# A fourth expert by seven products, the side product first, and stored first-layer remainders in a fused attention and mixture-of-experts kernel

## The chip, the cores and the metric

The kernel runs on one core of a Trainium2 chip. The metric is the device time of one execution in microseconds (us). The engines are TensorE (PE, with its weight loads as PEld), VectorE (DVE), ScalarE (ACT), GpSimd (POOL) and SyncE (SP), whose queue issues nearly all DMAs here.

## The reference

Three parts follow each other on 1152 tokens of 512 features, all in float32:

```python
# attention: 2 x 8 heads, 576 keys, head size 64; only the 32 largest scores of a row are kept
scores = scale * np.matmul(q, k.transpose(0, 1, 3, 2))
kth = np.partition(scores, -top_k, axis=-1)[..., -top_k:-top_k + 1]
attn = softmax(where(scores >= kth, scores, -1e9));  x = attn @ v
# first MoE: 8 experts, 512 -> 1024 -> 512, gates by 8 rounds of row and column normalization
for e in range(E):
    h = np.maximum(x @ w1[e], 0.0)
    out += P[:, e:e + 1] * (h @ w2[e])
# second MoE: one wide layer, 512 -> 2048 -> 512
h = x @ w_in
g = h * np.tanh(softplus(h))
return g @ w_out
```

## The kernel before

Every float32 operand of a matmul is split in two parts, a rounded one (`hi`, type fp32r) and the remainder (`lo`), and a product is made of three: hi by hi, hi by lo, lo by hi. ACT rounds (L542), POOL or DVE subtracts (L546). A weight expert is cut in eight pieces of 128 hidden features; a piece has a first-layer half `wraw0` and a second-layer half `wraw1`, 256 KB each, fetched through SP (L533) into three buffers each. The parts `wl0` have four buffers, `wl1` five.

The nine token tiles of 128 go in three chunks: (0, 1), (2, 3) and the last, (4 to 8). Attention produces the tiles; the experts of chunks 0 and 1 run on PE between the attention of later tiles. When attention has ended, the last chunk (640 tokens) is done. `moe_chunk` goes over its experts: the first `PLAIN` = 5 by `ffn_pass` (plain), the other three by `pair_pass`.

Plain: a piece makes h in two column groups of 256 and 384 (12 matmuls each, L805), ACT and DVE make `hh` (Relu, L633) and `hl` (L634) of them, and two pieces later come the second-layer products (L679): five tiles of three matmuls of 512 columns. The two groups take turns in two PSUM banks `mm1`, each free again when its `hl` has been made.

By pairs: two pieces are taken as a 2 x 2 block matrix and multiplied with the tokens by seven products of half size (`Seven`, `load_pair`, `pair_pass`). A product is six matmuls of 320 columns (L711). Banks `run` and `alt` are the two `mm1`; the bank `side` has the tag `misc`, one buffer, which the transposes `x2t` use too. The order of PE in a pair is: 11 by 11 into `run`, ACT copies it (p1, L723); 12 by 21 into `side`, DVE adds p1 (`total`, L729), Relu and `hl`; carried second-layer products of earlier pieces; s2 by t2 on top of `run`; carried; s3, then s1 into `alt`; carried; 22; carried; s4. POOL makes the block sums of the weights (L569 to L573) and their remainders.

The remainders of second-layer weights are made once for some experts (`KEPT`), written to DRAM (L549) in chunks 0 and 1 and loaded instead of made in the last chunk (L544): experts 1 to 3 in chunk 0, experts 4 to 7 in chunk 1.

Other work of the last chunk stands in DVE's queue between these: 32 spilled rows of chunks 0 and 1 are loaded (L1022) and accumulated (L826); the weights of the second MoE come as float64 and are turned into float32 by integer steps (`double_to_float`, L954 to L961, 32 conversions, loads `cx` L947, writes `w<-cb` L962); the operands t1 to t4 of the pairs are made (`steps`), for the last chunk on POOL, for the second MoE on DVE. PE's order is the order of the program text. The other engines' orders are chosen by the planner from priorities (`st`) and a simulated time line; `after` adds an order without a wait. `pace` ties conversions and rows to the newest `hl` by counts of finished pieces, `follow` ties the DVE steps of the second MoE's operand to totals and `hl`.

Behind the last chunk comes the second MoE, units of four and five tiles, all by `pair_pass` with the function Mish.

Of the kernel before, what the change touches and what calls it, by code (L numbers as in the profile page):

```python
# [19 lines left out]
P = 128  # L20
# [30 lines left out]
FILL_FROM = 9  # L51
PLAIN = 5
PAIRS_FROM, TURN_FROM = 78, 126
DOUBLES, LEFT_RATE, SUMS = (7, 0.8, 0.4), 0.4, (7, 1.15)
KEPT = ((1, 2, 3), (4, 5, 6, 7))
# [23 lines left out]
def attention_moe_moe2(ctx: ExitStack, tc: tile.TileContext, qT, kT, vm, vt, wg, wst, w64, out):  # L79
# [458 lines left out]
    def parts(a, tag, raw, eng, n=DM, key=None):  # L538
        hi, lo = (
            wp.tile([P, DM], F32R, tag=f"w{k}{a}", name=f"w{k}{a}_{tag}", bufs=(4, LAG + 3)[a])[:, :n] for k in "hl"  # L540
        )
        live["rounded"] = nc.scalar.activation(hi, raw, AF.Copy)  # L542
        if key in low:
            nc.sync.dma_start(lo.bitcast(F32), low[key])  # L544
            return hi, lo
        eng.tensor_sub(lo, raw, hi)  # L546
        if key is not None and ps_b is None:
            low[key] = dram.tile([P, DM], F32, tag=f"low_{key[0]}_{key[1]}", name=f"low_{key[0]}_{key[1]}")
            nc.sync.dma_start(low[key], lo.bitcast(F32))  # L549
        return hi, lo  # L550

    def load_piece(tag, p, key):
        engines = nc.gpsimd, nc.vector if ps_b is not None else nc.gpsimd
        return [parts(a, tag, fetch_raw(a, tag, p), eng, key=key if a else None) for a, eng in enumerate(engines)]
# [67 lines left out]
    class Relu:  # L622
# [8 lines left out]
        def first(self, ps, c0, m):  # L631
            h, l = self.hh[:, c0 : c0 + m], self.hl[:, c0 : c0 + m]
            nc.scalar.activation(h, ps, AF.Relu)  # L633
            live["hl"] = nc.vector.scalar_tensor_tensor(l, ps, 0.0, h, op0=ALU.max, op1=ALU.subtract)  # L634
            if carry:
                follow(LEFT_RATE, live["hl"])
# [48 lines left out]
    def pair_pass(tag, tiles, pieces, x, act_class, finish):  # L685
# [40 lines left out]
        def total(bank, u, act, half, last=True):  # L726
            with st("first"):
                c = bank if last else tp.tile([P, m], F32, tag="c", name=f"c_{tag}_{g}", bufs=2)
                follow(1, nc.vector.tensor_add(c, bank, u))  # L729
                act.first(c, half * m, m)  # L730
# [6 lines left out]
        for g in range(nf // 2):  # L737
            with st("prep" if carry else "moe"):
                keys = [(tag[1:].partition("e")[2], 2 * g + i) if tag[0] == "c" else None for i in range(2)]
# [4 lines left out]
            )  # L744
            product(run, "11", "11", True)
            p1 = kept(run, "p1")
            side = ps_b.tile([P, 512], F32, tag="misc", name=f"hs_{tag}_{g}")[:, :m]
            product(side, "12", "21", True)
            total(side, p1, acts[0], 0)
            yield  # L750
# [22 lines left out]
    def ffn_pass(tag, tiles, pieces, xhi, xlo, act_class, finish):  # L773
# [19 lines left out]
        for f, p in enumerate(pieces):  # L793
            with st("prep" if pending else "moe"):
                ci, _, e = tag[1:].partition("e")
                keep = ps_b is not None or int(e) in KEPT[int(ci)]
                (w1h, w1l), w2 = load_piece(f"{tag}_{f}", p, (e, f) if keep else None)
# [209 lines left out]
    def pace(n):  # L1007

        first, rate, later = DOUBLES
        due = (min(n, PLAIN * EP) - first) * rate + max(n - PLAIN * EP, 0) * later  # L1010
        for kind, ahead in (("rows", n - FILL_FROM + 1), ("doubles", due + 1)):
            for group in paced[kind][held[kind] : max(int(ahead), 0)]:
                for inst in group:
                    after(inst, live["hl"])
                held[kind] += 1
# [21 lines left out]
    for i, _ in enumerate(moe_chunk(len(CHUNKS) - 1)):  # L1037
        next(gating, None)
        if live["hl"] is not last:
            last = live["hl"]  # L1040
            pieces += 1 if pieces < PLAIN * EP else 2 / 3
            pace(pieces)
            while sums and drawn < (pieces - SUMS[0]) * SUMS[1]:
                after(sums.pop(0), last)
                drawn += 1
        if i >= TURN_FROM and (i - PAIRS_FROM) % 8 in TURNS:
# [93 lines left out]
```

## Time and profile before

| | |
|---|---|
| time, median of 3 runs | 1196.35 us (1196.2 to 1196.69) |
| profiled execution, time | 1198.0 us |
| its span, first to last instruction | 1196.1 us |
| granted clock over the span | 0.994 |
| PE / DVE / ACT / POOL busy | 1150.1 / 926.4 / 712.8 / 704.3 us |
| read from HBM / written | 174.11 / 38.54 MB |

Matmuls are pipelined, so the span of one is longer than the step from one start to the next; both are used below and named. Times in rows are us from the span's start. A row of the timeline is start, duration, engine, line, operation, tiles, shape, and in brackets the idle time before it with what released it.

### The profile page before, as it was taken

To read this page: it belongs to the slowest core of one execution; us is meant where nothing else is said; L and a number is where in the kernel's file an instruction comes from. 1 tells how busy PE (TensorE), PEld (TensorE's weight loads), DVE (VectorE), ACT (ScalarE), POOL (GpSimd) and SP (SyncE) were. 2 spreads that over 40 slices of the span, in tenths; PEclk is the share of its full clock that TensorE was granted. 3 is DMA by queue.
4 is the path that set the end of the run, shared out by engine and by line. 5 is a ranking of instruction groups with operands and counts; after the bars stand their busy time and mean duration, and the time that the engine had idled before them with its cause. 6 is when DMAs were issued, how large, how long until landed. Compare 5 with 4: busy or idle time off the path is not lost.

```text
span 1196.1 us, 21441 instructions
## 1 busy us (share of the span) xinstructions
PE 1150.1 (96%) x7251; PEld 1025.3 (86%) x7251; DVE 926.4 (77%) x1943; ACT 712.8 (60%) x1454; POOL 704.3 (59%) x607
## 2 busy tenths in 40 slices
PE   3788999999999999999999999999999999999998
PEld 2566888898888999889999999998898989889997
DVE  7999999999999999943578888777666457886442
ACT  5877777777777777754233333333455546767653
POOL 6544877888777787762223343433665576787651
PEclk9998999999999999999999999999999999999999
DMA  8358777657565677754257776766454332233201
GB/s 254 106 180 280 237 258 232 187 162 226 177 214 169 214 235 231 242 174 158 81 175 246 247 256 222 268 209 229 164 177 141 125 114 80 97 107 115 96 29 45
DMA packets 121967, 214.08 MB, mean 179 GB/s; under 512 B 16000, under 2 KB 26496, under 8 KB 121856
## 3 DMA queue, kind: packets, MB, share of 16 engines
q1 hardware_dynamic: 120560, 211.52, 54.5%
q8 instruction: 57, 0.93, 0.3%
q10 hardware_dynamic: 1296, 1.18, 0.3%
q14 instruction: 54, 0.44, 0.1%
HBM read 174.11 MB, written 38.54 MB: 178 GB/s over the span
## 4 chain that ended last, share of the span: by engine, by line
PE 87%; DVE 3%; DMA 1%; ACT 1%; issue 1%; POOL 0%; SPq 0%; ACTq 0%; POOLq 0%
PE y_c2e L679 17%; PE h_c2e L805 11%; PE y_d L679 8%; PE h_c1e L805 8%; PE y_c1e L679 8%; PE h_c0e L805 6%; PE y_c0e L679 6%; PE h_d L711 6%; PE h_c2e L711 5%; PE pv L358 3%; PE tr L335 2%; PE sc L236 2%; PE pv L365 1%; PE hs_d L711 1%; PE hs_c2e L711 1%
## 5 line engine op out<-in xcount | busy, mean ns | idle before, releaser
L546 POOL TENSOR_TENSOR wl_c1e<-wraw_c1e,wh_c1e 128x512 fp32r<-128x512 f32 x128 | 171.2, 1348 | 60.2 <-ACT wh_c1e L542 56.9
L546 POOL TENSOR_TENSOR wl_c0e<-wraw_c0e,wh_c0e 128x512 fp32r<-128x512 f32 x112 | 148.3, 1337 | 51.1 <-ACT wh_c0e L542 44.1
L264 DVE MAX8 top<-w 128x8 f32<-128x576 f32 x216 | 158.5, 748 | 1.0
L546 POOL TENSOR_TENSOR wl_c2e<-wraw_c2e,wh_c2e 128x512 fp32r<-128x512 f32 x40 | 53.2, 1330 | 171.6 <-ACT wh_c2e L542 163.7
L542 ACT ACTIVATE wh_c2e<-wraw_c2e 128x512 fp32r<-128x512 f32 x80 | 50.6, 632 | 143.6 <-PE y_c2e L679 76.9
L542 ACT ACTIVATE wh_c1e<-wraw_c1e 128x512 fp32r<-128x512 f32 x128 | 80.5, 629 | 47.3 <-PE y_c1e L679 22.1
L271 DVE MATCH_REPLACE8 w<-top,w 128x576 f32<-128x576 f32 x144 | 106.6, 741 | 0.0
L805 PE MATMUL h_c2e<-xh,wh_c2e 128*128 128x256 f32 (+1 forms) x320 | 98.7, 308 | 0.6 <-DVE hl_c2e L634 0.6
L805 PE MATMUL h_c2e<-xl,wh_c2e 128*128 128x256 f32 (+1 forms) x320 | 98.2, 307 | 0.0
L805 PE MATMUL h_c2e<-xh,wl_c2e 128*128 128x256 f32 (+1 forms) x320 | 98.1, 307 | 0.0
L542 ACT ACTIVATE wh_c0e<-wraw_c0e 128x512 fp32r<-128x512 f32 x112 | 70.4, 629 | 46.1 <-PE y_c0e L679 15.6
L634 DVE SCALAR_TENSOR_TENSOR hl_c2e<-h_c2e,hh_c2e 128x256 fp32r<-128x256 f32 (+1 forms) x104 | 50.6, 487 | 53.8 <-ACT hh_c2e L633 53.6
L236 PE MATMUL sc<-ks,q 128*128 128x288 f32 x320 | 66.0, 338 | 23.6 <-POOL ks L168 5.5
L236 PEld LDWEIGHTS sc<-ks,q 128*128 128x128 f32 x320 | 53.1, 211 | 34.1 <-ACT early L249 7.4
L679 PE MATMUL y_c2e<-wh_c2e,hl_c2e 128*128 128x512 f32 x200 | 78.7, 394 | 0.0
L679 PE MATMUL y_c2e<-wl_c2e,hh_c2e 128*128 128x512 f32 x200 | 78.4, 392 | 0.0
L679 PE MATMUL y_c2e<-wh_c2e,hh_c2e 128*128 128x512 f32 x200 | 78.4, 392 | 0.0
L805 PE MATMUL h_c1e<-xh,wh_c1e 128*128 128x256 f32 (+1 forms) x256 | 76.4, 298 | 0.0
L665 DVE TENSOR_TENSOR hl_d<-mg_d,hh_d 128x256 fp32r<-128x256 f32 (+1 forms) x64 | 50.5, 796 | 32.4 <-ACT hh_d L664 32.0
L805 PE MATMUL h_c1e<-xh,wl_c1e 128*128 128x256 f32 (+1 forms) x256 | 73.3, 286 | 0.0
L805 PE MATMUL h_c1e<-xl,wh_c1e 128*128 128x256 f32 (+1 forms) x256 | 73.2, 286 | 0.0
L805 PE MATMUL h_c0e<-xh,wh_c0e 128*128 128x256 f32 x224 | 66.7, 298 | 1.1 <-DVE hl_c0e L634 0.9
(532 smaller groups left out, 3963.0 us busy)
## 6 DMA issues: line engine op xcount, KB each, us to landing
wraw_c1e<-in_wst_dram SPq DMA_DIRECT2D x128, 256.0 KB, 3.1
wraw_c0e<-in_wst_dram SPq DMA_DIRECT2D x112, 256.0 KB, 3.2
wraw_c2e<-in_wst_dram SPq DMA_DIRECT2D x80, 256.0 KB, 3.3
cx<-in_w_dram SPq DMA_DIRECT2D x32, 512.0 KB, 5.0
yd<-ysp SPq DMA_DIRECT2D x32, 256.0 KB, 3.6
low<-wl_c1e SPq DMA_DIRECT2D x32, 256.0 KB, 2.7
yb<-yd SPq DMA_DIRECT2D x32, 256.0 KB, 3.6
wl_c2e<-low SPq DMA_DIRECT2D x32, 256.0 KB, 3.8
```

The source lines that it names most:

```text
L236: nc.tensor.matmul(halves[half], q[:, h % HG, :], ks[b, h][:, half * HS : (half + 1) * HS], start=(i == 0), stop=(i == len(terms) - 1),)
L264: top8 = nc.vector.max(g, src)
L271: nc.vector.match_replace(w, g, src, NEG)
L335: nc.tensor.transpose(tr[:, c, :], em[:, j * D + c * P :][:, :P], ident)
L358: nc.tensor.matmul(pv[i * D : (i + 1) * D, pair, c0:c1], vmain[b, pair][:, i, c, :], live["at", i][:, c, c0:c1], start=(c == 0), stop=False,)
L542: live["rounded"] = nc.scalar.activation(hi, raw, AF.Copy)
L546: eng.tensor_sub(lo, raw, hi)
L634: live["hl"] = nc.vector.scalar_tensor_tensor(l, ps, 0.0, h, op0=ALU.max, op1=ALU.subtract)
L665: follow(LEFT_RATE, nc.vector.tensor_sub(l, g, h))
L679: nc.tensor.matmul(y, h[:, j * P : (j + 1) * P], w, start=(start and k == 0), stop=(stop and k == len(products) - 1))
L711: nc.tensor.matmul(bank, a[:, cols], b[:, c, :], start=(start and c + k == 0), stop=(c == 1 and k == 2), skip_group_check=not start,)
L805: nc.tensor.matmul(ps, w[:, c * P : (c + 1) * P], x[:, c, c0 : c0 + m], start=(k == 0), stop=(k == 3 * NC - 1),)
```

## The change

- `PLAIN` goes from 5 to 4: the last chunk makes experts 0 to 3 plain and 4 to 7 by pairs, sixteen pairs instead of twelve.
- `KEPT` has two entries per chunk, for the first-layer and the second-layer half. New is the first-layer half of experts 1 to 3, written in chunk 1 and loaded in the last chunk.
- In a pair the side product (12 by 21) stands before 11 by 11. This holds for the second MoE too.
- In the last chunk the DVE steps for the second MoE's operand are tied to the first `hl` of a pair only, three of them (`LEFT_PAIR`); conversions too are tied to that `hl` (`lead`) in the pairs. In the second MoE the old rule stays.
- The counts at which rows, conversions and POOL's sums are due become plans of several stretches (`due`). The transposes of the first rows begin at pair 5 instead of pair 6 and stand at two places of a pair instead of three.

```diff
--- before.py
+++ after.py
@@ -48,11 +48,11 @@
 EARLY_FROM, EARLY_STEPS = 5, 9
 HOLD, RATE = 8, 0.25
 ALONE, ALONE_RATE = 1, 3.4
-FILL_FROM = 9
-PLAIN = 5
-PAIRS_FROM, TURN_FROM = 78, 126
-DOUBLES, LEFT_RATE, SUMS = (7, 0.8, 0.4), 0.4, (7, 1.15)
-KEPT = ((1, 2, 3), (4, 5, 6, 7))
+PLAIN = 4
+PAIRS_FROM, TURN_FROM = 62, 102
+ROWS, DOUBLES, SUMS = ((8, 1.25),), ((7, 0.8), (32, 0.475), (48, 0.28)), ((7, 1.4),)
+LEFT_RATE, LEFT_PAIR = 0.4, 3.0
+KEPT = (((), (1, 2, 3)), ((1, 2, 3), (4, 5, 6, 7)))
 TURNS = (2, 4, 6)
 
 
@@ -545,13 +545,13 @@
             return hi, lo
         eng.tensor_sub(lo, raw, hi)
         if key is not None and ps_b is None:
-            low[key] = dram.tile([P, DM], F32, tag=f"low_{key[0]}_{key[1]}", name=f"low_{key[0]}_{key[1]}")
+            low[key] = dram.tile([P, DM], F32, tag=f"low{key[0]}_{key[1]}_{key[2]}", name=f"low{key[0]}_{key[1]}_{key[2]}")
             nc.sync.dma_start(low[key], lo.bitcast(F32))
         return hi, lo
 
     def load_piece(tag, p, key):
         engines = nc.gpsimd, nc.vector if ps_b is not None else nc.gpsimd
-        return [parts(a, tag, fetch_raw(a, tag, p), eng, key=key if a else None) for a, eng in enumerate(engines)]
+        return [parts(a, tag, fetch_raw(a, tag, p), eng, key=key[a]) for a, eng in enumerate(engines)]
 
     def load_pair(tag, pa, pb, keys):
 
@@ -632,8 +632,6 @@
             h, l = self.hh[:, c0 : c0 + m], self.hl[:, c0 : c0 + m]
             nc.scalar.activation(h, ps, AF.Relu)
             live["hl"] = nc.vector.scalar_tensor_tensor(l, ps, 0.0, h, op0=ALU.max, op1=ALU.subtract)
-            if carry:
-                follow(LEFT_RATE, live["hl"])
 
     class LateRelu(Relu):
 
@@ -726,7 +724,9 @@
         def total(bank, u, act, half, last=True):
             with st("first"):
                 c = bank if last else tp.tile([P, m], F32, tag="c", name=f"c_{tag}_{g}", bufs=2)
-                follow(1, nc.vector.tensor_add(c, bank, u))
+                total = nc.vector.tensor_add(c, bank, u)
+                if tag[0] == "d":
+                    follow(1, total)
                 act.first(c, half * m, m)
 
         def carried():
@@ -736,17 +736,20 @@
 
         for g in range(nf // 2):
             with st("prep" if carry else "moe"):
-                keys = [(tag[1:].partition("e")[2], 2 * g + i) if tag[0] == "c" else None for i in range(2)]
+                keys = [(1, tag[1:].partition("e")[2], 2 * g + i) if tag[0] == "c" else None for i in range(2)]
                 w, w2 = load_pair(f"{tag}_{g}", pieces[2 * g], pieces[2 * g + 1], keys)
             acts = [act_class(f"{tag}_{2 * g + i}", n) for i in range(2)]
             run, alt = (
                 ps_m.tile([P, 512], F32, tag="mm1", name=f"h_{tag}_{g}_{i}", bufs=2)[:, :m] for i in range(2)
             )
+            side = ps_b.tile([P, 512], F32, tag="misc", name=f"hs_{tag}_{g}")[:, :m]
+            product(side, "12", "21", True)
             product(run, "11", "11", True)
             p1 = kept(run, "p1")
-            side = ps_b.tile([P, 512], F32, tag="misc", name=f"hs_{tag}_{g}")[:, :m]
-            product(side, "12", "21", True)
             total(side, p1, acts[0], 0)
+            if tag[0] == "c":
+                live["lead"] = live["hl"]
+                follow(LEFT_PAIR, live["hl"])
             yield
             yield from carried()
             product(run, "s2", "t2", False)
@@ -793,8 +796,8 @@
         for f, p in enumerate(pieces):
             with st("prep" if pending else "moe"):
                 ci, _, e = tag[1:].partition("e")
-                keep = ps_b is not None or int(e) in KEPT[int(ci)]
-                (w1h, w1l), w2 = load_piece(f"{tag}_{f}", p, (e, f) if keep else None)
+                kept = [ps_b is not None or int(e) in KEPT[int(ci)][a] for a in range(2)]
+                (w1h, w1l), w2 = load_piece(f"{tag}_{f}", p, [(a, e, f) if kept[a] else None for a in range(2)])
             act = act_class(f"{tag}_{f}", n)
             for c0, m in groups(n):
                 with st("moe"):
@@ -1004,15 +1007,19 @@
     paced = {"rows": [], "doubles": []}
     held = dict.fromkeys(paced, 0)
 
-    def pace(n):
-
-        first, rate, later = DOUBLES
-        due = (min(n, PLAIN * EP) - first) * rate + max(n - PLAIN * EP, 0) * later
-        for kind, ahead in (("rows", n - FILL_FROM + 1), ("doubles", due + 1)):
-            for group in paced[kind][held[kind] : max(int(ahead), 0)]:
-                for inst in group:
-                    after(inst, live["hl"])
-                held[kind] += 1
+    def due(plan, n):
+
+        ends = [at for at, _ in plan[1:]] + [n]
+        return sum(max(min(n, end) - at, 0) * rate for (at, rate), end in zip(plan, ends))
+
+    def pace(n, inst):
+
+        for kind, plan in (("rows", ROWS), ("doubles", DOUBLES)):
+            if n >= plan[0][0]:
+                for group in paced[kind][held[kind] : int(due(plan, n)) + 1]:
+                    for each in group:
+                        after(each, inst)
+                    held[kind] += 1
 
     def once_gated():
 
@@ -1036,14 +1043,15 @@
     last, pieces, drawn = live["hl"], 0, 0
     for i, _ in enumerate(moe_chunk(len(CHUNKS) - 1)):
         next(gating, None)
-        if live["hl"] is not last:
-            last = live["hl"]
-            pieces += 1 if pieces < PLAIN * EP else 2 / 3
-            pace(pieces)
-            while sums and drawn < (pieces - SUMS[0]) * SUMS[1]:
+        mark = live["hl" if pieces < PLAIN * EP else "lead"] if "lead" in live else live["hl"]
+        if mark is not last:
+            last = mark
+            pieces += 1 if pieces < PLAIN * EP else 2
+            pace(pieces, last)
+            while sums and drawn < due(SUMS, pieces):
                 after(sums.pop(0), last)
                 drawn += 1
-        if i >= TURN_FROM and (i - PAIRS_FROM) % 8 in TURNS:
+        if i >= TURN_FROM and (i - PAIRS_FROM) % 8 in TURNS[:2]:
             next(first_rows, None)
     for _ in first_rows:
         pass
```

## Rows read from the trace of the kernel before

**Rows 1.** Page, busy us (share) and instructions of each engine

```profile
PE 1150.1 (96%) x7251; PEld 1025.3 (86%) x7251; DVE 926.4 (77%) x1943; ACT 712.8 (60%) x1454; POOL 704.3 (59%) x607
```

**Rows 2.** Page, chain that ended last, shares by engine

```profile
PE 87%; DVE 3%; DMA 1%; ACT 1%; issue 1%; POOL 0%; SPq 0%; ACTq 0%; POOLq 0%
```

**Rows 3.** Stretch, us, busy of PE, PEld, DVE, ACT, POOL, clock, DMA, GB/s

```profile
616.46:824.29 207.83, 207.26 (x1172) 188.31 (x1171) 166.28 (x256) 74.36 (x144) 75.32 (x64) 1.00 0.74 243
834.60:995.00 160.40, 160.08 (x889) 143.97 (x888) 95.67 (x163) 83.18 (x169) 97.70 (x96) 1.00 0.43 140
```

**Rows 4.** Timeline of PE, the same product of two plain pieces

```profile
664.76 0.34 PE L805 MATMUL h_c2e<-xh,wl_c2e 128*128 128x384 f32 x1
671.66 0.34 PE L805 MATMUL h_c2e<-xh,wl_c2e 128*128 128x384 f32 x1
```

**Rows 5.** Timeline of PE, the same product of two pairs in a row

```profile
899.27 0.31 PE L711 MATMUL h_c2e<-xh,wh_c2e_s 128*128 128x320 f32 x1
912.36 0.31 PE L711 MATMUL h_c2e<-xh,wh_c2e_s 128*128 128x320 f32 x1
```

**Rows 6.** Timeline at the border from plain to pairs: SP, DVE, PE

```profile
802.10 0.32 SPq L962 DMA_DIRECT2D w<-cb  x1
...
809.06 0.43 DVE L954 TENSOR_SCALAR cb<-cx 128x512 uint32<-128x512 uint32 x1 [2.65 <-DMA w<-cb]
...
810.71 1.75 DVE L959 SCALAR_TENSOR_TENSOR cb<-cx,cb 128x512 f32<-128x512 uint32 x1
...
814.01 0.39 PE L805 MATMUL h_c2e<-xh,wh_c2e 128*128 128x256 f32 x1 [0.57 <-DVE hl_c2e L634]
```

**Rows 7.** Timeline at the transposes x2t, and in an undisturbed pair (929)

```profile
916.46 0.83 DVE L961 SCALAR_TENSOR_TENSOR cb<-cd,cb 128x512 f32<-128x512 f32 x1
917.12 0.31 PE L711 MATMUL h_c2e<-t_c,wl_c2e_s 128*128 128x320 f32 x1
917.21 0.48 DVE L634 SCALAR_TENSOR_TENSOR hl_c2e<-hs_c2e,hh_c2e 128x320 fp32r<-128x320 f32 x1
917.75 0.66 PE L985 MATMUL x2t<-ident,acc 128*128 128x128 f32 x4 [0.32 <-DVE hl_c2e L634]
...
929.79 0.31 PE L711 MATMUL hs_c2e<-xh,wl_c2e 128*128 128x320 f32 x1
931.20 0.49 DVE L634 SCALAR_TENSOR_TENSOR hl_c2e<-hs_c2e,hh_c2e 128x320 fp32r<-128x320 f32 x1 [0.50 <-ACT hh_c2e L633]
```

**Rows 8.** Timeline in the second MoE: ACT's copy p1, s2, and a late hl

```profile
1041.67 0.38 ACT L723 ACTIVATE p_d<-h_d 128x256 f32<-128x256 f32 x1
1042.14 0.46 PE L711 MATMUL h_d<-t_d,wh_d_s 128*128 128x256 f32 x2
...
1044.01 0.51 PE L679 MATMUL y_d<-wh_d_3a,hl_d 128*128 128x512 f32 x1 [0.47 <-DVE hl_d L665]
```

**Rows 9.** Groups by line, 615 to 782 us: busy, mean ns, idle

```profile
L546 POOL TENSOR_TENSOR wl_c2e<-wraw_c2e,wh_c2e 128x512 fp32r<-128x512 f32 x24 | 32.3, 1347 | 104.4 <-ACT wh_c2e L542 99.7 <-DMA wl_c2e<-low 4.7
...
L826 DVE SCALAR_TENSOR_TENSOR acc<-yb,gate,acc 128x512 f32<-128x512 f32 x20 | 22.0, 1099 | 0.0
L954 DVE TENSOR_SCALAR cb<-cx 128x512 uint32<-128x512 uint32 x20 | 18.0, 899 | 0.5 <-DMA w<-cb 0.5
```

**Rows 10.** SP's waits from 300 to 560 us (total, times, longest); a stage

```profile
SPq L549 <- POOL wl_c1e L546: 43.1, 31, 3.6
...
480.00:500.00 20.00, 20.00 (x153) 17.91 (x153) 19.90 (x51) 15.25 (x31) 15.91 (x13) 1.00 0.70 226
```

**Rows 11.** A plain piece; GB/s in 40 slices of 797 to 818 us

```profile
671.66:678.56 6.90, 6.90 (x40) 6.28 (x40) 5.98 (x10) 2.59 (x5) 2.16 (x2) 1.00 0.83 264
...
GB/s 0 0 0 0 0 86 195 218 269 234 234 191 152 320 371 406 410 417 398 367 351 215 129 23 90 273 265 363 328 359 273 156 257 359 156 324 211 129 238 351
```

**Rows 12.** DMA issues (KB each, median us to landing): 797 to 818 us, whole span

```profile
w<-cb SPq DMA_DIRECT2D x3, 256.0 KB, 6.1
...
w<-cb SPq DMA_DIRECT2D x32, 256.0 KB, 4.1
```

## The prediction

> **What bounds the kernel now.** I read the page first: TensorE (PE) is busy for 96% of the span [rows 1] and the chain that ended last is 87% PE [rows 2]. Then the table by stage, because the change touches one stage above all: from 616 to 824 us, four of the five plain experts of the last chunk, PE is busy 207.26 of 207.83 us; from 834.6 to 995 us, the three experts made in pairs, 160.08 of 160.40 us, both at a granted clock of 1.00 [rows 3]. So time can come out of this stretch in two ways only: fewer PE columns, or the few gaps. Matmul spans overlap, so I took the pitch from start to start and not the mean duration, and went through all PE starts from 560 us to the end for places where the next product began later than its pitch allows. Three are large enough to count and can be touched by the change: 0.57 us at 814 by the idle time of the row [rows 6], 0.48 us at 917 (six products in a row end their pitch of 0.147 at 917.27, the transposes begin at 917.75) [rows 7], 0.47 us at 1044 [rows 8]. Each was released by VectorE (DVE), not by a load. DVE is not the bound by its share (77%) [rows 1], but its queue is in order, so one late instruction holds up the remainder `hl` that PE needs.
>
> The profiled execution took 1198.0 us (span 1196.1, 1.9 around it), 1.65 above the median 1196.35. The terms are differences inside the span, so I take them off the median.
>
> **Expert 4 by pairs.** A plain piece takes 6.90 us from one first product to the same product of the next piece [rows 4], two pieces 13.80. A pair of pieces takes 13.09 us [rows 5]: 42 products of 320 columns instead of 24 of 256 and 24 of 384, with the same second layer. Saved: 0.71 us a pair, four pairs, **2.84 us**, all on PE, which has no gap there to hide it in. For comparison, the isolated gap that the Trainium skill gives per matmul (TensorE: Matmul & The Clock Gate, section Back-to-back issue gap: N/2.4 + 2.5 ns) would make this an estimate of 0.82 us a pair, 3.3 in all; the rows show 0.71 and decide. What the pairs add runs elsewhere: three totals on DVE, three copies and one and a half more roundings on ScalarE (ACT), POOL's half-width sums and remainders. The three pair experts show that these fit: in 160.4 us DVE has 95.67 busy, ACT 83.18, POOL 97.70 [rows 3]. Cost zero, hidden under 13.09 us of products per pair; if that cover fails, the price is that of the rivals.
>
> **Remainders of the first layer kept (experts 1 to 3).** It removes 24 POOL subtractions, 32.3 us by the row of this stretch [rows 9]. POOL was not late for PE there, so this gains nothing directly. It adds 24 writes of 256 KB in chunk 1 and 24 loads of 256 KB in the last chunk, all on SP's in-order queue. A write waits for POOL's subtraction, and what stands behind it, mostly the next raw weights, waits too. The same write is there already for experts 4 to 7: SP waited for POOL 31 times, 43.1 us in all, longest 3.6, and in 480 to 500 us, inside these writes, PE was busy 20.00 of 20.00 us [rows 10]. So 24 new ones (about 1.4 us of SP time each) cost between nothing and one such wait, 3.6 us, if a prefetch comes late; I take nothing, since the raw buffers are three deep and the row for the same case shows no PE gap.
> The loads: the fullest plain piece shows a DMA share of 0.83 at 264 GB/s [rows 11]. 256 KB more in 6.90 us are 38 GB/s, a quarter of a spilled row 9.5: 0.98 in such a piece. That is near full, not beyond: the engines moved over 350 GB/s for 3.7 us from 804.3 us on [rows 11]. Raw weights and remainders are fetched some pieces ahead, so I take zero and keep the collision as a rival.
>
> **New pace of DVE work.** Spilled rows go at 1.25 a piece instead of 1 and end near piece 33, as they must, since the transposes of the first rows start at pair 5 of 16. DVE was busy 5.98 of 6.90 us in a full piece [rows 11]. A quarter row at 1.10 us adds 0.27. Against that, the first step of a conversion averages 0.90 us [rows 9], and 0.43 where it ran undisturbed [rows 6]; with 24 POOL subtractions less, up to 0.47 of this may return. So 5.8 to 6.25 us a piece: it fits, cost zero. In the pairs the conversions come at 0.95, later 0.56 a pair instead of 0.8, and the 24 steps for the second MoE's first operand at 3 a pair over eight pairs. Both are now ordered behind the lead `hl` of a pair, the one that frees bank `misc`. At 917 us the last step of a conversion ran between the pair's total and that `hl` [rows 7]; tied behind it, it cannot. I take the **0.48** off.
>
> **Side product first.** The copy p1 can now start only when the second product of the pair has ended, and total, Relu and `hl` come one copy (0.44 us) later. In an undisturbed pair the side product's last matmul starts at 929.79 and ends 0.31 later, and `hl` ends at 931.69, 1.6 us after it [rows 7]. With a copy in front that is 2.05. The next product into `run` begins 1.2 us after that point, behind six second-layer products of 0.23 us; the copy ends at about 0.5. It is hidden with 0.7 us to spare. The transposes `x2t`, which share `misc`, come behind s2 (six of 0.147 us), 2.1 us after it: no slack is left. Two sit there in this chunk and two in the next. Bounds: 0 and 0.45 us each. I take 0.1 for the two in this chunk, **+0.2**, and nothing for the other two, where the bank is released by Mish on ACT, before `hl`. The bank `run` gets 0.88 us more to come free, but nothing waited for it: zero.
> The gap at the border from plain to pairs (814 us) and the one at 1044 us I leave as they are: conversions are as dense before the border as they were, and the second MoE's DVE queue isn't touched.
>
> Sum: -2.84 - 0.48 + 0.2 = -3.1 us; 1196.35 - 3.1 = **1193.2**.
>
> **Rivals.** *All three gaps go* (-2.84 - 0.57 - 0.48 - 0.47 = -4.4, 1192.0): the border moves to a stretch in which POOL has no remainders to make. Against it: the pair's own preparation on POOL begins before the border in any case. Chance 0.15.
> *Given back by the later chain*: at 1041.67 us p1 was late and ended 0.09 us before s2 began [rows 8]. If that lag belongs to the copy, it will end one product later, 0.7 us (six of 256 columns, in proportion to 320), and s2 waits 0.6 us. Two such pairs and two full waits at the transposes (0.9 instead of 0.2) make 1.9: 1195.1, up to 1196.5 if more pairs are late. Against it: ACT's queue, not the product, made p1 late there, and that queue doesn't move. Chance 0.22, nearly all within 0.2%.
> *Slower: the fuller DMA queue holds up DVE in the plain pieces.* At 809 us the first step of a conversion waited 2.65 us for the write of an earlier one, issued at 802.10; a later step then took 1.75 us, and `hl` behind it came 0.57 us too late for PE [rows 6]. The median landing of that write was 6.1 us in this burst against 4.1 over the run [rows 12]. With up to 0.98 of the DMA taken this can happen at many of the 20 conversions before the border. It decides from five such events on (2.84/0.57) and is slower by over 0.2% from ten (5.5/0.57); with ten to fifteen, 1198.9 to 1201.8. Against it: in the fullest piece, DMA share 0.83, PE had no gap [rows 11]. Chance 0.11. The Trainium skill (SBUF — State Buffer, section Who interferes with whom) says that a DVE instruction with two SBUF inputs is blocked by a GpSimd instruction that reads SBUF; the 1.75 us agree, as POOL worked then. By that rule the 24 subtractions taken off POOL speak for the change, and the preparation of four more pairs against it.
> That the reordering and tying do nothing at all leaves 2.84: 1193.5, inside the forecast.
>
> **How the numbers follow.** Forecast 0.52, all gaps gone 0.15, given back 0.22, slower 0.11. A measurement of this kernel can tell 0.2%, 2.4 us: faster means under 1193.96. Of the forecast 0.04 lies above that. Faster 0.48 + 0.15 = 0.63; same 0.22 + 0.04 = 0.26; slower 0.11. The range runs from 1191.4 (all gaps gone and a little) to 1197.0, past the giving back, and leaves out the slower rival and a bit below.
>
> **What would show it.** Right: a pair period of 13.1 us sixteen times in the last chunk; that chunk about 3 us shorter, with the stretch up to 560 us unchanged; 24 `wl` loads more and no POOL remainders in experts 1 to 3; no gap over 0.2 us at `x2t`. Wrong: PE gaps in plain pieces released by `hl` with a DVE wait for `w<-cb` before it (the DMA rival); gaps before s2 released by p1 (the later chain); a first 560 us longer by more than 0.5 us (SP's new writes).

## The result, and the profile after

The changed kernel takes **1207.67 us** (median of 6 runs, 1205.79 to 1209.83); the kernel before takes 1196.79 us in the same comparison. The ratio is 1.0089 [1.0076, 1.0102]: slower by about 11 us, where 3.1 us faster had been forecast. The profiled execution took 1207.27 us (span 1205.5, granted clock 0.994, as before).

The page of the changed kernel, first the busy times [rows 1], then the shares of the chain that ended last [rows 2]:

```profile
PE 1149.0 (95%) x7227; PEld 1019.9 (85%) x7227; DVE 935.2 (78%) x1955; ACT 718.5 (60%) x1474; POOL 692.1 (57%) x607
...
PE 80%; DVE 11%; ACT 3%; DMA 3%; issue 2%; POOL 1%; SPq 0%; ACTq 0%; POOLq 0%; DVEq 0%
```

PE has hardly less to do, but the chain leaves it more often: DVE's share went from 3 to 11%, ACT's from 1 to 3%. Where, the table by stage tells (columns as in [rows 3]; the last chunk's gating, three plain experts, and the pairs):

```profile
560.00:617.00 57.00, 54.87 (x328) 49.74 (x328) 34.36 (x104) 16.75 (x36) 27.61 (x32) 1.00 0.41 132
617.00:780.00 163.00, 163.00 (x921) 148.35 (x920) 121.43 (x208) 58.90 (x115) 15.28 (x15) 1.00 0.85 284
781.00:1001.00 220.00, 213.29 (x1170) 189.98 (x1169) 157.46 (x234) 108.05 (x226) 133.13 (x126) 1.00 0.48 154
```

PE stands for 2.1 us in the gating stage, not at all in the plain experts, and for 6.7 us in the pairs, where the kernel before stood for 0.32 us in 160.4 [rows 3]. From the starts of PE's products I made a ledger of every kernel of this study. "Plain" runs from the first product of the last chunk to the first one of its first pair, "pairs" from there to the first product of the second MoE, "second" from there to the start of the last product; one profiled execution each, us. Time is the median over all runs of the kernel; the ratio is to the kernel before, run beside it on the same chip. A ledger row is one execution, which can lie off its kernel's median: e1's is the one at 1203.54 us, e7's the one at 1202.98.

| kernel | plain | pairs | second | time | ratio, 95% interval |
|---|---|---|---|---|---|
| before (5 plain, 12 pairs) | 275.35 | 159.49 | 197.38 | 1196.79 | 1 |
| changed (4 plain, 16 pairs) | 222.07 | 219.93 | 200.29 | 1207.67 | 1.0089 [1.0076, 1.0102] |
| e1_side_back | 221.93 | 220.50 | 197.39 | 1207.93 | 1.0091 [1.0058, 1.0123] |
| e2_no_first_kept | 219.31 | 219.64 | 200.40 | 1205.76 | 1.0074 [1.0058, 1.0090] |
| e3_no_conv_border | 221.94 | 213.95 | 199.67 | 1201.85 | 1.0045 [1.0030, 1.0060] |
| e4_side_only (12 pairs) | 274.65 | 163.26 | 201.49 | 1204.49 | 1.0062 [1.0044, 1.0080] |
| e5_three_undone | 219.31 | 218.23 | 197.34 | 1198.26 | 1.0014 [1.0005, 1.0024] |
| e6_kept_only (12 pairs) | 277.09 | 159.41 | 198.54 | 1199.56 | 1.0030 [1.0017, 1.0043] |
| e7_side_back_border | 221.90 | 219.61 | 197.32 | 1200.57 | 1.0032 [1.0019, 1.0045] |
| e8_four_old_pace | 219.31 | 218.00 | 198.22 | 1199.11 | 1.0026 [1.0014, 1.0038] |
| e9_no_late_conv | 219.36 | 210.93 | 197.60 | 1191.59 | 0.9959 [0.9944, 0.9974] |
| e10_kept_two (12 pairs) | 274.88 | 159.21 | 198.48 | 1195.98 | 0.9994 [0.9984, 1.0003] |
| e11_more_plain | 226.30 | 214.69 | 197.00 | 1200.88 | 1.0036 [1.0023, 1.0049] |
| e12_pool_steps | 230.22 | 219.00 | 197.35 | 1209.00 | 1.0099 [1.0083, 1.0116] |

Read against e9, in which PE's longest wait in these three parts is 0.32 us, the changed kernel loses 2.7 us in plain, 9.0 in the pairs, 2.7 in the second MoE. Waits of PE are given below from start to start, beyond the usual step of the matmul before. They come out about 0.15 us longer than the idle time in a row's brackets, because a matmul's span is longer than its step; for the same reason the busy times above show less than the 9.0 us.

**The pairs.** Groups of the conversion's six steps on DVE, changed kernel, 781 to 1000 us (columns as in [rows 9]; lines 957 to 964 are 954 to 961 of before), then the first step in the three pair experts of before, 834.6 to 995 us:

```profile
L964 DVE SCALAR_TENSOR_TENSOR cb<-cd,cb 128x512 f32<-128x512 f32 x12 | 14.4, 1204 | 0.6
L962 DVE SCALAR_TENSOR_TENSOR cb<-cx,cb 128x512 f32<-128x512 uint32 x12 | 13.9, 1161 | 0.4
L960 DVE SCALAR_TENSOR_TENSOR ca<-cx,cb 128x512 uint32<-128x512 uint32 x12 | 12.9, 1071 | 0.3
L963 DVE TENSOR_TENSOR cb<-ca,cb 128x512 f32<-128x512 f32 x12 | 9.5, 795 | 0.3
L961 DVE TENSOR_SCALAR cb<-ca 128x512 uint32<-128x512 uint32 x12 | 9.1, 762 | 0.3
L957 DVE TENSOR_SCALAR cb<-cx 128x512 uint32<-128x512 uint32 x12 | 8.9, 743 | 0.0
```

```profile
L954 DVE TENSOR_SCALAR cb<-cx 128x512 uint32<-128x512 uint32 x5 | 3.5, 697 | 0.0
```

Twelve conversions run in the pairs instead of six, counting in both kernels the one that lies astride the border (its first step falls ahead of the stretch of before, hence x5). They take 5.74 us each (the sum of the six means), 68.7 us of DVE. What this does to PE at a border between two pair experts, on the timeline of DVE, ACT, POOL and PE of the changed kernel:

```profile
837.34 0.49 DVE L634 SCALAR_TENSOR_TENSOR hl_c2e<-hs_c2e,hh_c2e 128x320 fp32r<-128x320 f32 x1 [0.50 <-ACT hh_c2e L633]
837.74 0.77 DVE L957 TENSOR_SCALAR cb<-cx 128x512 uint32<-128x512 uint32 x1
...
843.50 1.60 DVE L964 SCALAR_TENSOR_TENSOR cb<-cd,cb 128x512 f32<-128x512 f32 x1
845.02 0.48 DVE L727 TENSOR_TENSOR c_c2e<-h_c2e,u_c2e 128x320 f32<-128x320 f32 x1
845.42 1.39 DVE L829 SCALAR_TENSOR_TENSOR acc<-y_c2e,gate,acc 128x512 f32<-128x512 f32 x2
846.74 1.50 DVE L634 SCALAR_TENSOR_TENSOR hl_c2e<-c_c2e,hh_c2e 128x320 fp32r<-128x320 f32 x1
848.16 0.74 DVE L829 SCALAR_TENSOR_TENSOR acc<-y_c2e,gate,acc 128x512 f32<-128x512 f32 x1
848.82 0.47 DVE L634 SCALAR_TENSOR_TENSOR hl_c2e<-h_c2e,hh_c2e 128x320 fp32r<-128x320 f32 x1
...
840.65 0.44 ACT L721 ACTIVATE u_c2e<-h_c2e 128x320 f32<-128x320 f32 x1 [0.24 <-PE h_c2e L709]
...
846.61 1.29 POOL L546 TENSOR_TENSOR wl_c2e_s<-wraw_c2e_1b,wh_c2e_s 128x512 fp32r<-128x512 f32 x1 [2.05 <-PE h_c2e L709]
...
849.35 0.41 PE L709 MATMUL h_c2e<-xh,wh_c2e 128*128 128x320 f32 x1 [1.77 <-DVE hl_c2e L634]
```

Behind the lead `hl` comes a whole conversion (six steps, to 845.1). The total `c` needs the copy u (done at 841.09) and product s1 (its last matmul ends at 841.49), and runs at 845.02, some 3.5 us late. At this border the old expert's sums must be accumulated too (`acc`, 0.7 us each), and three of them stand ahead of the `hl` that frees bank `run`. Between them runs the `hl` of c, which takes 1.50 us itself, beside POOL's subtraction (last section). PE waits 1.92 us here, 1.82 at 907.61, 1.12 at 961.89, each followed by a late p1 (0.67, 0.66, 0.66). The other waits in the pairs are 0.54, 0.37 and 0.37 us at x2t. Together these make 8.1 of the 9.0 us.

No DVE instruction of these pairs waits 0.2 us or more for a DMA. In the six microseconds around the first border, and in those around 905 and 959 us, DVE is busy for 17.93 of 18.00 us:

```profile
844.00:850.00 6.00, 4.23 (x24) 3.55 (x24) 6.00 (x9) 2.14 (x5) 2.77 (x3) 1.00 0.55 192
```

**Gating.** First the changed kernel, then before: POOL's groups from 560 to 617 us and one step of DVE, for the changed kernel also POOL beside that step and the wait of PE:

```profile
L610 POOL TENSOR_TENSOR x_c<-xh,xl 128x320 f32<-128x320 f32 x8 | 7.3, 948 | 0.1
...
L546 POOL TENSOR_TENSOR wl_c2e<-wraw_c2e,wh_c2e 128x512 fp32r<-128x512 f32 x4 | 5.2, 1297 | 21.4 <-ACT wh_c2e L542 13.0 <-DMA wraw_c2e<-in_wst_dram 8.4
...
595.74 3.37 POOL L610 TENSOR_TENSOR x_c<-xh,xl 128x320 f32<-128x320 f32 x4
...
598.34 0.87 DVE L513 TENSOR_TENSOR gate<-gate,cr 128x72 f32<-128x72 f32 x1
...
600.81 0.41 PE L507 MATMUL cs<-gate,ones 128*128 128x72 f32 x2 [1.00 <-DVE gate L503]
```

```profile
L546 POOL TENSOR_TENSOR wl_c2e<-wraw_c2e,wh_c2e 128x512 fp32r<-128x512 f32 x8 | 10.4, 1295 | 45.9 <-ACT wh_c2e L542 42.8 <-DMA wraw_c2e<-in_wst_dram 3.1
L610 POOL TENSOR_TENSOR x_c<-xh,xl 128x320 f32<-128x320 f32 x2 | 1.7, 880 | 0.0
...
592.82 0.23 DVE L513 TENSOR_TENSOR gate<-gate,cr 128x72 f32<-128x72 f32 x1
```

Before, POOL's subtractions of the next weights waited 42.8 us for ACT, and POOL's sums x_c, which stand behind them in its queue, waited with them. Four of these subtractions are gone, so the sums run early, in the middle of the gating, and some of DVE's small steps beside them take several times as long (0.87 for 0.23 us). PE waits 0.34, 1.12 and 1.16 us for the gate.

**Second MoE.** ACT and PE, changed kernel; compare [rows 8]:

```profile
1071.75 0.61 ACT L542 ACTIVATE wh_d<-wraw_d_7a 128x512 fp32r<-128x512 f32 x1
1072.27 0.36 ACT L721 ACTIVATE p_d<-h_d 128x256 f32<-128x256 f32 x1
...
1072.69 0.50 PE L709 MATMUL h_d<-t_d,wh_d_s 128*128 128x256 f32 x2 [0.92 <-ACT p_d L721]
```

p1 now stands behind a rounding in ACT's queue, and s2 waits 1.09 us for it (0.80 at 1004.67). In the last unit a pair takes 13.20 to 13.24 us, against 13.05 to 13.10 with the old order (e1).

### The profile page after: what moved, and what is told of

Its sections match the earlier page's. It is cut to its first block, busy times and chain, and to the rows that moved or that the text cites. A ratio compares the mean times of both kernels' runs of the same rounds, so it can differ in the third digit from the quotient of the medians.

```text
span 1205.5 us, 21534 instructions
## 1 busy us (share of the span) xinstructions
PE 1149.0 (95%) x7227; PEld 1019.9 (85%) x7227; DVE 935.2 (78%) x1955; ACT 718.5 (60%) x1474; POOL 692.1 (57%) x607
## 4 chain that ended last, share of the span: by engine, by line
PE 80%; DVE 11%; ACT 3%; DMA 3%; issue 2%; POOL 1%; SPq 0%; ACTq 0%; POOLq 0%; DVEq 0%
PE y_c2e L677 16%; PE h_c2e L808 9%; PE y_d L677 7%; PE h_c1e L808 7%; PE y_c1e L677 7%; PE h_c0e L808 6%; PE y_c0e L677 6%; PE h_d L709 6%; PE h_c2e L709 5%; PE pv L358 2%; DVE top L264 2%; PE sc L236 2%; PE tr L335 2%; DMA kraw<-in_kT_dram 2%; DVE w L271 2%
## 5 line engine op out<-in xcount | busy, mean ns | idle before, releaser
L542 ACT ACTIVATE wh_c2e<-wraw_c2e 128x512 fp32r<-128x512 f32 x64 | 40.5, 633 | 116.3 <-PE y_c2e L677 63.0
L634 DVE SCALAR_TENSOR_TENSOR hl_c2e<-h_c2e,hh_c2e 128x256 fp32r<-128x256 f32 (+1 forms) x96 | 46.9, 489 | 59.4 <-ACT hh_c2e L633 59.3
L569 POOL TENSOR_TENSOR ws_c2e<-wraw_c2e_0a,wraw_c2e_0b 128x256 f32<-128x256 f32 x4 | 3.0, 752 | 148.5 <-DMA wraw_c2e_0b<-in_wst_dram 148.5
L663 DVE TENSOR_TENSOR hl_d<-mg_d,hh_d 128x256 fp32r<-128x256 f32 (+1 forms) x64 | 47.2, 737 | 50.3 <-ACT hh_d L662 49.9
L808 PE MATMUL h_c2e<-xh,wh_c2e 128*128 128x256 f32 (+1 forms) x256 | 78.9, 308 | 0.0
L808 PE MATMUL h_c2e<-xl,wh_c2e 128*128 128x256 f32 (+1 forms) x256 | 78.5, 307 | 0.0
L808 PE MATMUL h_c2e<-xh,wl_c2e 128*128 128x256 f32 (+1 forms) x256 | 78.5, 307 | 0.0
L633 ACT ACTIVATE hh_c2e<-h_c2e 128x256 fp32r<-128x256 f32 (+1 forms) x96 | 41.2, 429 | 41.8 <-PE h_c2e L808 24.4
L808 PE MATMUL h_c0e<-xl,wh_c0e 128*128 128x256 f32 x224 | 63.1, 282 | 0.0
L808 PE MATMUL h_c0e<-xh,wl_c0e 128*128 128x256 f32 x224 | 63.0, 281 | 0.0
```

Of the source, the lines that this page charges most:

```text
L663: follow(LEFT_RATE, nc.vector.tensor_sub(l, g, h))
L808: nc.tensor.matmul(ps, w[:, c * P : (c + 1) * P], x[:, c, c0 : c0 + m], start=(k == 0), stop=(k == 3 * NC - 1),)
```

## The experiments

The theory after the comparison: three causes add up, the conversions in the pairs, the gating under POOL's sums, and the later chain of the side product. The main rivals: one of them alone makes it all, or the loss is the DMA queue, as the prediction had it.

### One part undone at a time

**e1_side_back**: the changed kernel with 11 by 11 in front again.

```diff
-            side = ps_b.tile([P, 512], F32, tag="misc", name=f"hs_{tag}_{g}")[:, :m]
-            product(side, "12", "21", True)
             product(run, "11", "11", True)
             p1 = kept(run, "p1")
+            side = ps_b.tile([P, 512], F32, tag="misc", name=f"hs_{tag}_{g}")[:, :m]
+            product(side, "12", "21", True)
```

> The changed kernel with 11 by 11 in front of the side product again; all else as changed. Pile-up theory (a conversion tied behind the lead hl, POOL's pair preparation and the five accumulations of an expert that ends meet in DVE's queue at pairs 4, 8 and 12): the order of the two products is a lesser part. The waits for p1 go (0.7 us three times in the pairs, 2.7 us in the second MoE) and the lead hl comes about 1 us earlier; the waits for hl at the three borders stay at 1 us or more: 1202 to 1204.5. Rival (the side product first is the cause of nearly all): 1196 to 1199. Gating stretch unchanged, PE gaps of about 2.3 us before 601 us.

The second MoE is back at 197.39, so that loss is the side product's. But the pairs don't gain (220.50; PE waits 1.96, 2.77 and twice 0.9 us for `hl`, at other pairs), and the time is no better: neither range was met. With the lead `hl` at another place the conversions collide with something else. The four runs lie between 1203.54 and 1211.13 us, and the ledger is that of the one at 1203.54: what the others lose, no trace shows. Some 1.5 us of these pairs are not a wait. After the 2.77 us the granted clock is 0.50 for 3.4 us, 1.2 instead of 2.4 GHz, and a product of 320 columns takes a step of 0.27 instead of 0.147 us:

```profile
959.00:962.50 3.50, 3.50 (x14) 3.31 (x13) 2.17 (x5) 1.67 (x4) 1.06 (x2) 0.51 0.50 166
```

The same stands behind long waits in e7 (795.9 to 799.3 us), e11 (762.6 to 766.0) and, beginning within the wait, e12 (797.2 to 804.0). It doesn't stand behind every one: e5's wait of 1.90 us at 793.06 and the changed kernel's of 1.92 were followed by none.

**e2_no_first_kept**: the first-layer half of experts 1 to 3 made again.

```diff
-KEPT = (((), (1, 2, 3)), ((1, 2, 3), (4, 5, 6, 7)))
+KEPT = (((), (1, 2, 3)), ((), (4, 5, 6, 7)))
```

> The changed kernel without stored first-layer remainders (the second-layer ones stay). Theory: POOL's queue loses what held its sums back, so they ran in the gating stretch, and DVE's small gating steps were slowed; without the change the 2.3 us of PE gaps before 601 us go, as does the gap of 1.3 us at 354 us if SP's new writes made it; the gaps in the pairs stay: 1203.5 to 1205.5. Rival (the DMA load of the plain pieces carries over into the pairs): 1199 or less.

All three gating waits are gone and nothing else moved by more than 0.3 us in the ledger: plain 222.07 to 219.31. The time, 1205.76, is 0.3 us above the expected range.

**e3_no_conv_border**: as many conversions, but none tied to the first pair of the last three experts; one at each other pair until all are made.

```diff
-                for group in paced[kind][held[kind] : int(due(plan, n)) + 1]:
+                want = int(due(plan, n)) + 1
+                if kind == "doubles" and n > PLAIN * EP:
+                    pair = int(n - PLAIN * EP) // 2 - 1
+                    want = 21 + sum(1 for k in range(pair + 1) if k == 0 or k % 4)
+                for group in paced[kind][held[kind] : want]:
```

> The changed kernel with one conversion per pair at pairs 0 to 13 except 4, 8 and 12, where an expert ends; all 32 conversions are still made. Pile-up theory: the hl waits at pairs 5, 9 and 13 and the p1 waits behind them go, 6 to 8 us: 1199.5 to 1202. Rival (the five accumulations and the later lead alone are enough): gaps stay over 1 us each, 1205 or more.

As the theory had it: 6.0 us out of the pairs. The row of the pairs:

```profile
781.00:1001.00 220.00, 218.41 (x1205) 195.51 (x1204) 157.76 (x240) 112.94 (x234) 135.65 (x132) 1.00 0.50 158
```

DVE is as busy as in the changed kernel (157.76 against 157.46 us), and PE 5.1 us more. What counts between these two is behind which instruction a conversion stands, not how much DVE has to do.

**e5_three_undone** (e1, e2 and e3 together) and **e7_side_back_border** (e1 and e3).

> The changed kernel with three parts undone at once: 11 by 11 first again, no stored first-layer remainders, no conversion at pairs 4, 8 and 12. Four experts by pairs, conversions and the second MoE's operand still tied to the lead hl. Theory (three separate losses, each gone with its part; the 2.84 us of PE columns remain): gating stretch without gaps, second MoE as before (196.7 us from its first side product to the end), sixteen pairs in about 212 us, 1193 to 1196. Rival (four pair experts overload DVE whatever the order): pairs over 215 us, 1198 or more.

> The changed kernel with 11 by 11 first again and no conversion at pairs 4, 8 and 12; stored first-layer remainders stay. Theory: what e3 gave (6 us in the pairs) and what e1 gave in the second MoE (3.6 us) add up, the gating gap stays: 1196.5 to 1199. Rival (with the lead hl at the old place the conversions collide elsewhere): 1201 or more.

Plain and second MoE are clean in e5, but the theory missed in both: the pairs take 218.23 and 219.61. In e5 the rival's numbers held; e7, at 1200.57, lies between its two. With the old order in the pair, the places that e3 chose are bad ones; in e5 a conversion stands ahead of total and `hl` in the first pair (PE waits 1.90 us), and 0.89 us is lost in three more. In e7 the first pair's wait of 1.90 us is followed by 3.4 us at a granted clock of 0.50, some 1.5 us more. Neither of the two placements tried suits the old order.

### One part alone

**e4_side_only**: the kernel before with the side product first (the reverse of e1's diff).

> The kernel before with the side product in front of 11 by 11 and nothing else. Theory: 2.5 to 3 us of waits for p1 in the second MoE, up to 1 us at the transposes and borders of the pairs: 1199 to 1201. Rival (the order is the cause of nearly all): 1204 or more. Rival (the order costs nothing without the tied work): 1196.5 to 1197.5.

Larger than expected: 3.8 us in the twelve pairs and 4.1 in the second MoE. It is as dear alone as the rival "cause of nearly all" said, but e1 shows that it isn't the only cause. One of its waits, of 1.46 us, in the second MoE:

```profile
1102.90 0.42 PE L711 MATMUL h_d<-t_d,wh_d_s 128*128 128x320 f32 x1 [1.30 <-ACT p_d L723]
```

**e6_kept_only** and **e10_kept_two**: the kernel before with the kept first-layer remainders, for experts 1 to 3 and for 2 and 3 only.

```diff
-KEPT = ((1, 2, 3), (4, 5, 6, 7))
+KEPT = (((), (1, 2, 3)), ((1, 2, 3), (4, 5, 6, 7)))
...
```

This is e6; in e10 the line is `KEPT = (((), (1, 2, 3)), ((2, 3), (4, 5, 6, 7)))`. What is left out here is the changed kernel's handling of two halves.

> The kernel before with stored first-layer remainders of experts 1 to 3 and nothing else. Theory (POOL's sums lose what held them back and run beside the gating steps of DVE; SP's writes add a gap at 355 us): PE gaps of 2.3 to 2.8 us before 601 us, perhaps 1.3 at 355: 1198.5 to 1200.5. Rival (the gating gap comes from the faster pace of the sums): 1196 to 1197.5.

> e6 with first-layer remainders kept for experts 2 and 3 only; POOL subtracts for expert 1 again. Theory (what stands in POOL's queue between the sums holds them back from the gating stretch): the PE gaps of 2.6 us before 601 us go, 1196 to 1198. Rival (loads or writes of remainders on SP's queue delay the gating): at least 1.5 us of these gaps stay, 1198.5 or more.

Both came out as the theory had it. The gating stage of e6, then of e10:

```profile
560.00:617.00 57.00, 54.88 (x327) 49.95 (x326) 34.33 (x104) 16.91 (x36) 25.42 (x29) 1.00 0.41 130
```

```profile
560.00:617.00 57.00, 57.00 (x340) 52.34 (x339) 32.67 (x106) 18.31 (x38) 13.15 (x11) 1.00 0.38 119
```

With expert 1's subtractions back, POOL is held as before (13.15 us busy for 25.42) and PE doesn't stand. So storing and loading for experts 2 and 3 cost nothing; what costs is that POOL is free during the gating. e10 takes expert 1's stores and loads out as well. That these are not the cause is read from the rows above: PE's waits are for the gate, whose steps run long beside the sums. e10 is the same as before: the stored remainders bring nothing where POOL was not late.

**e8_four_old_pace**: the kernel before with four plain experts, the counts shifted to match and POOL's sums a little faster.

```diff
-PLAIN = 5
-PAIRS_FROM, TURN_FROM = 78, 126
-DOUBLES, LEFT_RATE, SUMS = (7, 0.8, 0.4), 0.4, (7, 1.15)
+PLAIN = 4
+PAIRS_FROM, TURN_FROM = 62, 110
+DOUBLES, LEFT_RATE, SUMS = (7, 0.8, 0.4), 0.4, (7, 1.4)
```

> The kernel before with the fourth expert by pairs alone: old product order, old remainders, conversions tied to any hl at the old rates (the 32 fit in the last pair), rows at one a piece, POOL's sums at 1.4 a piece so that they end before the first pair. Theory: 2.84 us of PE columns come out, and what the old pacing meets at the borders goes off that: 1193.5 to 1197. Rival (four pair experts by themselves overload DVE): 1199 or more.

The rival held: the fourth pair expert, with the conversions that it pushes into the pairs, makes the kernel slower by itself, by 0.26%, most of it in the pairs (218.00, five waits of 0.5 to 1.8 us for `hl`).

### Is the saving there, and what takes it?

**e9_no_late_conv**: e5 without its last twelve conversions; the second MoE takes the first six weight pieces again in place of the last six.

```diff
-            for p in range(NPIECE2):
+            for p in range(10):
...
+            w32.extend(w32[:6])
```

> e5 with the conversions of the last six of the 16 weight pieces of the second MoE left out (12 conversions; those pieces are computed with the first six pieces' weights), so that none stands in the pairs. Theory (the conversions that the shorter plain stretch pushes into the pairs, 12 against 5 before at 5.7 us of DVE each, make the gaps, and the four pair experts as such do not): sixteen pairs in 211.5 to 213.5 us instead of 218.1, 1192 to 1194.5. Rival (accumulations at the borders and POOL's preparation are enough): pairs over 216 us, 1196 or more.

The pairs of e5, then of e9:

```profile
781.00:1001.00 220.00, 215.12 (x1181) 191.70 (x1180) 158.44 (x233) 112.48 (x231) 134.71 (x131) 1.00 0.47 153
```

```profile
781.00:1001.00 220.00, 220.00 (x1228) 198.40 (x1227) 102.36 (x175) 112.69 (x231) 128.67 (x135) 1.00 0.36 116
```

PE runs through, sixteen pairs in 210.93 us, even less than expected, and the kernel is faster than before by 0.41%. Last chunk 430.29 us against 434.84: 4.55 less, where the four pairs' 2.84 and the gaps at 814 and 917 us (0.57 and 0.48) make 3.9; the other 0.7 us is not traced. So the seven products save what the rows said, and the conversions in the pairs eat it (7.3 us between e5 and e9). e9 leaves out their loads and writes as well. That DVE and not the DMA is what counts is read from the waits of e5: PE's are for DVE, and no DVE instruction of its pairs waits 0.2 us or more for a DMA.

**e11_more_plain**: the changed kernel with e1, e10's `KEPT`, and 25 conversions before the border instead of 21. **e12_pool_steps**: the same, and the last two steps of these 25 on POOL.

```diff
-ROWS, DOUBLES, SUMS = ((8, 1.25),), ((7, 0.8), (32, 0.475), (48, 0.28)), ((7, 1.4),)
+ROWS, DOUBLES, SUMS = ((8, 1.25),), ((7, 0.8), (16, 1.1)), ((7, 1.4),)
...
+                    want = 25 + sum(1 for k in range(pair + 1) if k % 4)
```

In e12 further:

```diff
-        nc.vector.tensor_add(b, a.bitcast(F32), b)
-        nc.vector.scalar_tensor_tensor(b, sq, TINY2, b, op0=ALU.is_ge, op1=ALU.mult)
+        if len(paced["doubles"]) <= 25:
+            nc.gpsimd.tensor_add(b, a.bitcast(F32), b)
+            nc.gpsimd.tensor_scalar(sq, sq, TINY2, None, op0=ALU.is_ge)
+            nc.gpsimd.tensor_mul(b, b, sq)
...
```

> A version drawn from the runs: four experts by pairs, 11 by 11 first, remainders kept for experts 2 and 3, conversions at 1.1 a piece from piece 16 on, so that 25 are done before the border and the other 7 stand in pairs 1, 2, 3, 5, 6, 7 and 9, none where an expert ends. Theory (conversions are cheap beside plain pieces without POOL's subtractions, dear beside pairs): pairs in 213 to 215 us, 1192.5 to 1195.5. Rival (DVE at over 90% in experts 2 and 3 makes gaps in the plain pieces): 1196 or more.

> e11 with the last two steps of the first 25 conversions on POOL (an addition, a comparison and a product there) instead of DVE. Theory (DVE's queue is what the conversions overfill, in plain pieces as in pairs; POOL has room in experts 1 to 3): a conversion takes 2.8 us of DVE instead of 4.2, the gaps of 4 us and more in e11's plain pieces go, pairs as in e11 at about 214.5: 1193 to 1196. Rival (POOL's added work locks DVE's operands and delays POOL's sums, which the first pair needs): plain gaps stay or a gap opens at the first pair, 1199 or more.

Both rivals held by their times. e11 has its pairs at 214.69, as expected, but its plain part lost 7 us, some 1.5 of them at a granted clock of 0.50 behind its longest wait. DVE and PE at that wait:

```profile
757.21 0.43 DVE L957 TENSOR_SCALAR cb<-cx 128x512 uint32<-128x512 uint32 x1 [4.04 <-DMA w<-cb]
...
761.02 0.41 DVE L634 SCALAR_TENSOR_TENSOR hl_c2e<-h_c2e,hh_c2e 128x256 fp32r<-128x256 f32 x1
...
761.48 0.39 PE L808 MATMUL h_c2e<-xh,wh_c2e 128*128 128x256 f32 x1 [2.46 <-DVE hl_c2e L634]
```

This is the prediction's DMA rival, at a higher rate of conversions: the first step waits 4.04 us for the write of an earlier one, and `hl` behind it comes late. DVE's share was not the reason: 137.44 of 165 us (83%), where the rival had put it over 90%. e12 moves DVE's work to POOL and is worse; 615 to 780 us of e11, then of e12:

```profile
615.00:780.00 165.00, 161.28 (x895) 145.21 (x894) 137.44 (x224) 59.39 (x115) 47.11 (x41) 0.99 0.84 282
```

```profile
615.00:780.00 165.00, 157.49 (x878) 141.32 (x876) 133.04 (x175) 58.43 (x113) 135.54 (x106) 1.00 0.82 278
```

49 DVE instructions fewer save DVE 4.4 us only, while POOL gets 88 us more. Behind these 165 us its first pair waits 2.99 us for the copy u, and 6.8 us at a granted clock of 0.50 begin there.

## Why the prediction was wrong, point by point

- **The saving on PE was right.** Pairs take 13.05 to 13.10 us wherever nothing is late, and e9 gets the gain. The term of -2.84 stands.
- **"Cost zero, hidden under 13.09 us of products per pair" failed**, and with it the forecast. It took DVE's 95.67 us of 160.4 [rows 3] for what sixteen pairs would have; they have 157.46 of 220. The step behind it is "in the pairs the conversions come at 0.95, later 0.56 a pair instead of 0.8": it compared two rates. The old rate ran dry after five conversions, since 27 of the 32 had begun in five plain experts; with four, 21 have, and eleven are left. This is what the runs showed in place of "cost zero": 9.0 us lost in the pairs, and 7.3 between e5 and e9. A count of one group in the three stages of the kernel before (x20 in [rows 9] for some three plain experts, x5 in the pairs) would have told it. A conversion also costs more there: 5.74 us of DVE by the six means, where the pairs of before had 5.04.
- **Tied behind the lead `hl`** (-0.48): the conversion did leave the place ahead of that `hl`, and took the place ahead of the next total. The step asked what the tie forbids and not what it lets in front. x2t waits 0.54, 0.37 and 0.37.
- **Side product first** (+0.2) was mis-sized: 2.9 us in the second MoE (200.29 against 197.39 in e1), and 3.8 in twelve pairs by e4. The rival *given back by the later chain* named the place, s2 behind p1 [rows 8], but also the argument against it: "ACT's queue, not the product, made p1 late there, and that queue doesn't move". ACT's order did move: p1 now comes behind a rounding.
- **Remainders kept** (0): 2.6 us in the gating (three waits; e2, e6). I counted POOL's subtractions as work that goes, and didn't ask what they held back. The 24 new writes on SP cost nothing, as put: SP's waits for POOL rose from 43.1 us [rows 10] to 69.2, and the last chunk begins no later (559.12 against 559.45).
- **The DMA rival** didn't happen: DMA share 0.85 at 284 GB/s in the plain experts and PE 163.00 of 163.00 us; e11 shows that its mechanism exists one step further on. The gap at 814 us, which I left as it was, went away.

The sum by parts (2.6 gating, 9.0 pairs, 2.9 second MoE), less e9's gain of 4.3 us from the chunk's first product to the end, gives 10.2 us. The profiled executions differ by 10.1 there and by 9.4 over the span, the medians by 10.9. The parts aren't independent, as e1, e5 and e7 show. Open: a wait of 1.48 us for ACT at 356 us, in the changed kernel and e3 only; and how the 9.0 us split between the number of conversions and their slower steps.

## What to carry to other kernels

When a stage gets longer and another shorter, count the side work of each stage anew instead of comparing its rates; "it fits by share" is no cover on an in-order queue, where one long item ahead of a short one that PE needs is enough. Before taking work off an idle engine, look at what stands behind it in that engine's queue and where that will now run. A tie behind an instruction is also a permission to stand ahead of the next one.

## What the runs showed of the hardware

DVE steps slow down beside POOL, whole instructions at a time, and only some forms of them. In e5, `hl` made from the tile c (two SBUF inputs) begins 0.08 us after a subtraction of POOL and takes 1.56 us, about as if it began when POOL ends (790.94); a second `hl` made from a PSUM bank takes 0.47 beside the same kind of subtraction:

```profile
789.73 1.56 DVE L634 SCALAR_TENSOR_TENSOR hl_c2e<-c_c2e,hh_c2e 128x320 fp32r<-128x320 f32 x1
...
792.53 0.47 DVE L634 SCALAR_TENSOR_TENSOR hl_c2e<-h_c2e,hh_c2e 128x320 fp32r<-128x320 f32 x1
...
789.65 1.29 POOL L546 TENSOR_TENSOR wl_c2e_s<-wraw_c2e_1b,wh_c2e_s 128x512 fp32r<-128x512 f32 x1 [2.05 <-ACT wh_c2e_s L542]
...
792.06 0.72 POOL L546 TENSOR_TENSOR wl_c2e_s<-wraw_c2e_1a,wh_c2e_s 128x256 fp32r<-128x256 f32 x1 [1.12 <-ACT wh_c2e_s L542]
```

This agrees with the Trainium skill (SBUF — State Buffer, section Who interferes with whom), by which a DVE instruction with two SBUF inputs contends with a GpSimd instruction that reads SBUF, and one with at most one SBUF input, outside the two-port modes, does not. In the gating a step with a single input slowed down too (`cr` plus a constant, 128x8, 0.85 us at 596.62 in the changed kernel, 0.17 at 595.37 before); whether it ran in such a mode, no run shows. Over a stage it adds up: from 617 to 780 us e5 has DVE busy 138.93 us for 210 instructions with POOL at 67.68, the changed kernel 121.43 for 208 with POOL at 15.28.

```profile
617.00:780.00 163.00, 163.00 (x922) 148.30 (x921) 138.93 (x210) 58.92 (x116) 67.68 (x61) 1.00 0.76 255
```

PE stood in neither, so these 17.5 us were worth nothing there. That POOL's work alone makes them is argued from the two stretches, not tested by itself.
